# A linear-attention block beside a squared-ReLU layer: the last 64 query features taken from the keys' products, denominators by transposition

## The chip, the cores and the metric

The kernel runs on one core of a Trainium2 chip. A core has a matrix engine (TensorE, PE in the profile, with its weight loads as PEld), a vector engine (VectorE, DVE), a scalar engine (ScalarE, ACT), GpSimd (POOL) and a queue processor (SyncE, SP), which here only issues transfers. Each runs its own list of instructions in order and waits on semaphores for the others. Transfers are moved by 16 DMA engines. The metric is the device time of one execution in microseconds (us); lower is better.

## The reference, cut to what matters

There are S = 2048 rows x of D = 448 features. Two branches read the same x and are mixed by a gate per row:

```python
g = sigmoid((x * gate_w).sum(-1, keepdims=True))
# a: linear attention, 16 heads of 28 features
q, k, v = (x @ wqkv) split into three, each in 16 heads
phi = lambda t: where(t > 0, t + 1, exp(t)) + 1e-6
pq, pk = phi(q), phi(k)
kv  = einsum("hsd,hse->hde", pk, v)
z   = sum over s of pk                       # 28 sums for each head
num = einsum("hqd,hde->hqe", pq, kv)
den = einsum("hqd,hd->hq", pq, z) + 1e-6
a = (num / den) @ wo
# b: relu(x @ w1 + b1) ** 2 @ w2 + b2, 1792 hidden features
out = g * a + (1 - g) * b
```

## The kernel before

**Precision.** Operands are split into a high part, rounded for TensorE, and the low remainder; each product of matrices is two or three products on TensorE (high by high, high by low, low by high). The split is an ACT pass for the high part (`split_hi`, L65) and a VectorE subtraction for the low part (`split_lo`, L72). The 448 features fill three chunks of 128 partitions, and a fourth chunk of 64 carries high and low halves together, so a contraction over x takes 3 + 3 + 3 + 2 = 11 products.

**Order of the work.** The rows are four blocks (NB) of 512, each of four tiles of 128. Phase 1 walks blocks 0 to 3 and, for each, seven steps f of the hidden layer. A step does `up` (11 products of 512 columns, L229, into h_ps), `down` for the step before (12 products of 448 columns, L254, into o_ps) and one further piece: in steps 0 to 3 `keys` of one tile (11 products into k_ps, then phi in `first`, and splits and key sums in `rest`), in steps 4 to 6 `gram`, which sums phi(k) times x. Phase 2 walks the blocks in the order 3, 0, 1, 2, again in seven steps for the other half of the hidden layer. Its further pieces are `queries` (q_ps), the denominators, `scaled` (queries divided by them, and split), and `attention` (a_ps). In the first block of phase 2 also `kv_product` and `m_product` make the matrix m_s = kv times wo, whose parts are moved into place by transfers on POOL's queue (L442 to L444).

TensorE, ACT and VectorE keep the order in which the code calls them. Steps that use a finished product are put on the list `todo` and run at the start of the next step (`run_todo`). For SP and POOL a scheduler orders the instructions by when it reckons them ready. Most temporary tiles share 15 slots of the pool `work` (`slot`); a load waits on SP until its slot is free. Accumulators are banks of PSUM: `bank` alternates between two, h_ps and m_ps share two others, o_ps has four.

**Queries.** q_of puts 512 query features in four chunks of 128 partitions: 32 partitions for four heads. The last 64 features fill chunk 3 twice over, each once per half of a 32-group, so that high and low parts can be contracted together later (`split_last`). In `queries` chunks 0 to 2 take 11 products each and chunk 3 takes 7, whose result for half of a group lacks a low term; `swap` copies it out (L472), sends the halves of each 32-group to each other's place by 4 transfers on SP and 4 on POOL (L475), and `join` adds them. Chunk 3 is made first for a block, chunks 0, 1, 2 follow. After each chunk, phi gives pq, and ds gathers pq times zc, the key sums laid out by partition.

**Denominators.** `split_den` splits ds (dh, dl); `denominators` multiplies both by hm, a 128 x 128 mask that sums over the partitions of a head (d_ps, two products). ACT copies the result out with 1e-6 added (L494), and VectorE takes four reciprocals of 128 columns (L498).

**Key sums.** Each key tile's phi(k) is added up on POOL (L326) in ksum, [128 rows, 448]. `key_sums` puts it in the order of the query chunks (zk); in `kv_product` TensorE sums over the 128 rows with a column of ones (z_ps, four calls, eight products), and VectorE copies them to zc.

Of the kernel before, what the change touches and what calls it, by code (L numbers as in the profile page):

```python
# [30 lines left out]
def gated_mix_kernel(ctx: ExitStack, tc: tile.TileContext, xw, xt, xn, wk, wq, wv, wo, w1a, w1b, w2, b1, b2, gw,  # L31
                     hmask, kvmask, halves, out):
# [102 lines left out]
    def new_w1(h, g):  # L135
        n, a, z = ((TB, 0, 16), (3 * P, 48, 0))[g]
# [25 lines left out]

    wk_raw = {}

    def load_wk(c):
        wk_raw[c] = slot([P, D], F, f"wkr{c}")
        load(wk_raw[c], wk[c])
# [25 lines left out]
    ones = keep.tile([P, 2], F, name="ones")  # L193
    logit = keep.tile([P, NT], F, name="logit")
    gate = keep.tile([P, 2, NT], F, name="gate")
    zc = keep.tile([P, 4], F, name="zc")
# [10 lines left out]
    hm = keep.tile([P, 8 + P], R, name="hm")[:, 8:]  # L207
    dve.memset(ones, 1.0)
# [7 lines left out]
    hs = {}  # L216

# [72 lines left out]
    def keys(t, leave=0):  # L290
        b, i = divmod(t, 4)
        if t < 2:
            ps = (acc_p, mm_p)[t].tile([P, 512], F, name=f"k_ps{t}", tag=("acc", "mm")[t])
        else:
            ps = bank(f"k_ps{t}")
        terms = [term for c in range(4) for term in terms_x(*xs[b], slice(i * P, (i + 1) * P), wk_s, slice(0, D), c)]
        for n, (a, m) in enumerate(terms):
            owed.append((ps[:, :D], a, m, n == 0, n == len(terms) - 1))
# [48 lines left out]
    wq_s = keep.tile([P, 7 * TB], R, name="wq_s")  # L347
    wq_s = wq_s.rearrange("p (c n) -> p c n", c=7)
    wq_raw = {}

    def load_wq(c):
        wq_raw[c] = slot([P, TB], F, f"wqr{c}")
        load(wq_raw[c], wq[c])
# [3 lines left out]
    def split_wq(c):  # L357
        raw = wq_raw.pop(c)
        split_hi(act, wq_s[:, c], raw)
        if c < 3:  # L360
            split_lo(dve, wq_s[:, 4 + c, :384], raw[:, :384], wq_s[:, c, :384])
        else:
            split_lo(dve, wq_s[64:, 3, :384], raw[64:, :384], wq_s[64:, 3, :384])
        second = [t[:, 384:].rearrange("p (j r) -> p j r", j=NJ)[:, :, 16:] for t in (wq_s[:, c], raw)]
        split_lo(dve, second[0], second[1], second[0])
# [4 lines left out]
    zks = []  # L370

    def key_sums():
        zk = slot([P, 4, NJ, 32], F, "zk")
        ks = ksum.rearrange("p (j k) -> p j k", j=NJ)
        pool.memset(zk[:, 3], 0.0)
        pool.tensor_copy(zk[:, :3], ks[:, :, :96].rearrange("p j (c r) -> p c j r", c=3))
        pool.tensor_copy(zk[:, 3, :, :16], ks[:, :, 96:])
        zks.append(zk)
        act.activation(gate[:, 0], logit, AF.Exp, scale=-1.0)
        dve.tensor_scalar_add(gate[:, 0], gate[:, 0], 1.0)  # L380
        dve.reciprocal(gate[:, 0], gate[:, 0])
        dve.tensor_scalar(gate[:, 1], gate[:, 0], -1.0, 1.0, op0=ALU.mult, op1=ALU.add)
# [11 lines left out]
    def kv_product():  # L394
        kv_ps = bank("kv_ps")
        z_ps = mm_p.tile([P, 512], F, name="z_ps", tag="mm")
        for c in range(4):
            pe.matmul(z_ps[:, 2 * c:2 * c + 2], zks[0][:, c].rearrange("p j r -> p (j r)"), ones, start=True,  # L398
                      stop=True)
        dve.tensor_copy(zc, z_ps[:, 0:8:2])  # L400
# [31 lines left out]
    def m_product(j):  # L432
# [10 lines left out]
        pool.dma_start(out=m_s[p:p + 16, 3], in_=m[96:112, 0])  # L443
        pool.dma_start(out=m_s[p + 16:p + 32, 3], in_=m[112:, 1])  # L444


    pq, qs, den = {}, {}, {}

    def queries(b, c):
        ps = bank(f"q_ps{b}_{c}")  # L450
        xh, xl = xs[b]
        cols = slice(c * P, (c + 1) * P)
        if c < 3:
            products(ps, terms_w(xh, xl, wq_s, cols))
        else:
            products(ps, [(wq_s[:, i, cols], x[:, i]) for i in range(4) for x in ((xh, xl) if i < 3 else (xh,))])
        e = slot([P, TB], F, f"qe{b}_{c}")
        r = slot([P, TB], F, f"qr{b}_{c}")
        v = slot([P, TB], F, f"qv{b}") if c == 3 else None
        pq[b, c] = e  # L460

        def after():
            phi(ps if c < 3 else v, e, r, e)
# [5 lines left out]

        def swap():  # L470

            act.copy(v, ps)  # L472
            for p in range(0, P, 32):
                load(r[p:p + 16], v[p + 16:p + 32])
                pool.dma_start(out=r[p + 16:p + 32], in_=v[p:p + 16])  # L475
            return [join]

        def join():
            dve.tensor_tensor(v, v, r, op=ALU.add)
            after()  # L480
        return [swap if c == 3 else after]

    def split_den(b):
        den[b, "h"], den[b, "l"] = slot([P, TB], R, f"dh{b}"), slot([P, TB], R, f"dl{b}")
        total = den.pop((b, "s"))
        split_hi(act, den[b, "h"], total)
        split_lo(dve, den[b, "l"], total, den[b, "h"])

    def denominators(b):
        ps = bank(f"d_ps{b}")  # L490
        products(ps, [(hm, den.pop((b, "h"))), (hm, den.pop((b, "l")))])
        den[b, "r"] = rec = slot([P, TB], F, f"rec{b}")

        act.activation(rec, ps, AF.Copy, bias=1e-6)  # L494

        def part_(i):
            for j in range(2 * i, 2 * i + 2):
                dve.reciprocal(rec[:, j * P:(j + 1) * P], rec[:, j * P:(j + 1) * P])  # L498
        return [lambda: part_(0), lambda: part_(1)]

    def scaled(b, c):
        p = pq.pop((b, c))
        h = late.tile([P, TB], R, name=f"qh{b}_{c}", tag="q", bufs=NLATE)
        lo = late.tile([P, TB], R, name=f"ql{b}_{c}", tag="q", bufs=NLATE)
        qs[c] = (h, lo)
        dve.tensor_tensor(p, den[b, "r"], p, op=ALU.mult)
        if c < 3:
            split_hi(act, h, p)
            split_lo(dve, lo, p, h)
        else:  # L510
            split_last(h, lo, p, half)
# [18 lines left out]
    def run_todo():  # L530
        now, todo[:] = sorted(todo, key=lambda step: step.__name__ == "join"), []
# [33 lines left out]
    wk_s = keep.tile([P, 7, D], R, name="wk_s", tag="wkm", bufs=1)  # L565
# [53 lines left out]
    for b in range(1, NB):  # L619
        for f in range(NH):  # L620
# [36 lines left out]
            if b == 2:  # L657
# [4 lines left out]
                if f == 5:  # L662
                    raw = slot([P, P], F, "hmr")
                    pool.dma_start(out=raw, in_=hmask)
                    split_hi(act, hm, raw)
                    load(half, halves)
            if b == 3:
# [19 lines left out]
    for n, b in enumerate(order):  # L687
        then = order[n + 1] if n + 1 < NB else None
        for f in range(NF - NH, NF):
            fl = f - NH  # L690
            run_todo()
            if fl == (0 if n else 4) and n != 1:
                split_den(b)
            up(b, f)
            if then is not None and n and fl < 2:
# [32 lines left out]
            else:  # L728
                down(order[n - 1], NF - 1)
                for i in range(4):  # L730
                    if n == 1:
                        attention(order[0], i)
                        if i == 1:
                            split_den(b)
                    finish(order[n - 1], i)
            if n == 0:
                if fl in (2, 3):
                    m_product(fl - 2)
                if fl < 4:
                    todo += queries(b, (3, 0, 1, 2)[fl])  # L740
                if fl == 0:
# [5 lines left out]
                    m_s = keep.tile([P, 7, D], R, name="m_s", tag="wkm", bufs=1)  # L747
# [7 lines left out]
                for c in ((0,), (1, 2, 3))[fl - 5] if fl >= 5 else ():  # L755
                    scaled(b, c)
# [3 lines left out]
                if fl == 4:  # L760
                    todo += denominators(b)
            else:
                if fl == 0:
                    todo += denominators(b)
                if 2 <= fl < 4:
                    scaled(b, 2 * fl - 4)
                    scaled(b, 2 * fl - 3)
# [74 lines left out]
```

## Time and profile before

| | |
|---|---|
| device time, three runs | 434.67, 435.01, 435.04 us; median 435.01 |
| span of the profiled execution | 432.7 us |
| between span and median | 2.3 us |
| TensorE busy | 428.9 us, 2058 products |
| VectorE, ACT, POOL busy | 284.7, 174.8, 72.0 us |
| moved by DMA | 29.11 MB in 18411 packets |

The profile shows one execution. Busy times are unions of an engine's instructions. Matmuls are pipelined, so that their records overlap: the mean of a group is the duration of one product and not the distance from one to the next. That distance is read from the chain that ended last, which gives start, length and count of each run of products. A name such as "k_ps" stands for a tile with its buffer numbers left out; "L254" is a line of the kernel, which can be that of a helper.

### The profile page before, as it was taken

The page shows a single profiled execution, that of the slowest core. Times are in us where ns is not written, and L with a number is a line of the kernel's source. Part 1 is how long each engine was busy: PE and PEld are TensorE (multiplying, and loading weights), DVE is VectorE, ACT ScalarE, POOL GpSimd, SP SyncE. Part 2 cuts the span into 40 slices and gives each one's busy share as a digit, 9 for nine tenths or more (in the row PEclk, how much of TensorE's full clock was granted, in tenths as well). Part 3 has the DMA queues.
Part 4 walks back from the last instruction along what each step waited for, and adds up shares of the span by engine and source line. Part 5 has one row for each costly group of instructions (what it writes and reads, how often), then busy time and mean ns, then how long its engine had stood idle before and what let it go on. Part 6 is the DMA issues. An engine that isn't in the chain of part 4 may idle for free.

```text
span 432.7 us, 5576 instructions
## 1 busy us (share of the span) xinstructions
PE 428.9 (99%) x2058; PEld 380.6 (88%) x2058; DVE 284.7 (66%) x464; ACT 174.8 (40%) x304; POOL 72.0 (17%) x93
## 2 busy tenths in 40 slices
PE   9999999999999999999999999999999999999997
PEld 6889999898989899898898888988888888888986
DVE  5999518843499337884459777887653966457624
ACT  6855324521346133453145543444433534233421
POOL 0055006500065002540010441000100001000000
PEclk9999999999999999999999999999999999999999
DMA  8842302120232211223245321130101401002002
GB/s 284 240 134 63 96 0 71 24 68 5 65 89 63 68 45 48 66 59 110 65 117 144 72 63 38 63 120 0 26 0 46 139 0 27 0 0 86 0 2 85
DMA packets 18411, 29.11 MB, mean 67 GB/s; under 512 B 2896, under 2 KB 12736, under 8 KB 18384
## 3 DMA queue, kind: packets, MB, share of 16 engines
q1 hardware_dynamic: 16480, 26.46, 20.1%
q0 software_dynamic: 1760, 2.20, 2.3%
q8 instruction: 16, 0.26, 0.3%
q14 instruction: 11, 0.09, 0.1%
q10 hardware_dynamic: 144, 0.10, 0.1%
HBM read 22.43 MB, written 3.67 MB: 60 GB/s over the span
## 4 chain that ended last, share of the span: by engine, by line
PE 99%; DVE 0%; issue 0%
PE h_ps L229 32%; PE o_ps L254 31%; PE q_ps L84 8%; PE a_ps L84 8%; PE g_ps L84 8%; PE k_ps L254 8%; PE kv_ps L404 1%; PE warm_ps L177 1%; PE m_ps L84 1%; PE d_ps L84 0%; PE last L84 0%; PE h_ps L549 0%; PE z_ps L398 0%; DVE last L786 0%
## 5 line engine op out<-in xcount | busy, mean ns | idle before, releaser
L254 PE MATMUL o_ps<-w,hh 128*128 128x448 f32 x444 | 127.9, 362 | 0.0
L229 PE MATMUL h_ps<-xh,w 128*128 128x512 f32 x390 | 124.7, 390 | 0.0
L254 PEld LDWEIGHTS o_ps<-w,hh 128*128 128x128 f32 x444 | 83.2, 187 | 7.6
L229 PE MATMUL h_ps<-xl,w 128*128 128x512 f32 x224 | 86.7, 389 | 0.0
L229 PEld LDWEIGHTS h_ps<-xh,w 128*128 128x128 f32 x390 | 73.1, 188 | 14.7 <-DVE w L72 0.4
L254 PE MATMUL o_ps<-w,hl 128*128 128x448 f32 x222 | 80.4, 362 | 0.0
L233 ACT ACTIVATE hr<-h_ps,b_s 128x512 f32<-128x512 f32 x56 | 38.1, 680 | 85.8 <-PE h_ps L229 80.3
L69 DVE CAST hh<-hr 128x512 fp32r<-128x512 f32 x56 | 23.5, 420 | 61.3 <-ACT hr L234 61.1
L229 PEld LDWEIGHTS h_ps<-xl,w 128*128 128x128 f32 x224 | 42.0, 188 | 7.9
L254 PEld LDWEIGHTS o_ps<-w,hl 128*128 128x128 f32 x222 | 41.6, 188 | 3.7
L72 DVE TENSOR_TENSOR hl<-hr,hh 128x512 fp32r<-128x512 f32 x56 | 39.6, 707 | 3.4
L72 POOL TENSOR_TENSOR nl<-xnr,nh 128x384 fp32r<-128x384 f32 x16 | 17.2, 1075 | 119.0 <-ACT nh L65 118.9
L234 ACT ACTIVATE hr<-hr 128x512 f32<-128x512 f32 x56 | 35.4, 632 | 1.8
L84 PE MATMUL q_ps<-xh,wq_s 128*128 128x512 f32 x100 | 33.0, 389 | 0.0
L84 PE MATMUL a_ps<-m_s,qh 128*128 128x448 f32 x112 | 32.7, 362 | 0.0
L254 PE MATMUL k_ps<-wk_s,xh 128*128 128x448 f32 x112 | 32.7, 361 | 0.0
L475 POOL DMA_DIRECT2D qr<-qv x16 | 7.9, 503 | 124.3 <-ACT qv L472 94.5
L72 DVE TENSOR_TENSOR pl<-r,ph 128x448 fp32r<-128x448 f32 x16 | 23.7, 1479 | 0.0
L326 POOL TENSOR_TENSOR ksum<-ksum,r 128x448 f32<-128x448 f32 x15 | 23.3, 1554 | 1.1 <-DVE r L288 1.1
L84 PE MATMUL q_ps<-xl,wq_s 128*128 128x512 f32 x60 | 23.3, 389 | 0.0
L254 PE MATMUL k_ps<-wk_s,xl 128*128 128x448 f32 x64 | 23.2, 363 | 0.0
L84 PE MATMUL a_ps<-m_s,ql 128*128 128x448 f32 x64 | 23.2, 362 | 0.0
(118 smaller groups left out, 571.0 us busy)
## 6 DMA issues: line engine op xcount, KB each, us to landing
xr<-in_xt SPq DMA_DIRECT2D x27, 256.0 KB, 2.7
xnr<-in_xn SPq DMA_DIRECT2D x16, 224.0 KB, 2.6
out<-out SPq DMA_DIRECT2D x15, 224.0 KB, 2.0
w2r<-in_w SPq DMA_DIRECT2D x14, 224.0 KB, 2.7
w1r<-in_w1a SPq DMA_DIRECT2D x7, 256.0 KB, 2.8
w1r<-in_w1b SPq DMA_DIRECT2D x8, 192.0 KB, 3.3
m_s<-m POOLq DMA_DIRECT2D x12, 112.0 KB, 2.5
wqr<-in_wq SPq DMA_DIRECT2D x4, 256.0 KB, 2.7
```

The source lines that it names most:

```text
L69: eng.tensor_copy(hi, src)
L72: eng.tensor_tensor(lo, src, f32(hi), op=ALU.subtract)
L84: pe.matmul(out_ps, a, b, start=(i == 0), stop=(i == n - 1))
L177: pe.matmul(warm_ps[:, :256], warm[:, :P], warm, start=True, stop=True)
L229: pe.matmul(ps, a, m, start=(c == 0 and n == 0), stop=(c == 3 and n == 1))
L233: act.activation(r, ps, AF.Relu, bias=b1_s[:, f:f + 1])
L234: act.activation(r, r, AF.Square)
L254: pe.matmul(ps, a, m, start=start, stop=stop)
L326: pool.tensor_tensor(ksum, ksum, p, op=ALU.add)
L404: pe.matmul(kv_ps[:JE, js], wv_s[c][:, js], gsum[c][:, js], start=(c == 0), stop=(c == 3))
L475: pool.dma_start(out=r[p + 16:p + 32], in_=v[p:p + 16])
```

## The change

Four things are done in another way.

1. The weights of the last 64 query features stand beside the key weights: wk_s gets 512 columns in place of 448, and a key product gives a tile of rows by 448 key features and 64 query features. In `first`, VectorE transposes the 64 query columns in 32 x 32 blocks (tile q3), and SP writes the result to memory (q_d, 32 KB for each tile of rows). `load_v` later reads a block of 512 rows back, in four transfers in runs of 32 numbers (128 bytes), as a tile with features on partitions, each feature on two adjacent partitions. `queries` uses it as chunk 3. The seven products of chunk 3, `swap` and `join` are gone, and wq has 384 columns.
2. The partitions are permuted: a head's features lie on eight adjacent partitions in each chunk.
3. Denominators: ds is transposed on VectorE in 32 x 32 blocks, so that the eight partitions of a head become eight adjacent columns; VectorE reduces them to 64 columns, adds 1e-6 and takes one reciprocal of 64 columns; ACT spreads each over eight columns; VectorE transposes back. The mask hm and its products are gone.
4. Key sums: zk is transposed and reduced on VectorE, the result goes to memory in one transfer (zd) and comes back in four (z4), and `add_z`, one step later, adds the four parts into zc. z_ps is gone.

Chunk 3 comes last in a block of phase 2 (in the first block, first), `denominators` is called one step earlier or directly, and `scaled` does two chunks at a time with the first one's low part taken after the second one's multiplication. In the diff, whose cuts are lines of "...", some paddings of tiles are changed too.

```diff
     def load_wk(c):
-        wk_raw[c] = slot([P, D], F, f"wkr{c}")
+        wk_raw[c] = slot([P, TB], F, f"wkr{c}")
...
-        terms = [term for c in range(4) for term in terms_x(*xs[b], slice(i * P, (i + 1) * P), wk_s, slice(0, D), c)]
+        terms = [term for c in range(4) for term in terms_x(*xs[b], slice(i * P, (i + 1) * P), wk_s, slice(0, TB), c)]
...
         def first():
-            phi(ps[:, :D], e, r, p)
+            act.activation(e, ps[:, :D], AF.Exp)
+            dve.tensor_scalar(r, ps[:, :D], 0.0, 1e-6, op0=ALU.max, op1=ALU.add)
+            q = tmp.tile([P, 2, 32], F, name=f"q3_{t}", tag="q3", bufs=4)
+            dve.transpose(q.rearrange("p a s -> p (a s)"), ps[:, D:])
+            dve.scalar_tensor_tensor(p, e, 1.0, r, op0=ALU.min, op1=ALU.add)
+            qd = q_d[b].tile([4, P, 2, 32], F, name=f"qd{b}") if i == 0 else q_t[b]
+            q_t[b] = qd
+            load(qd[i], q)
...
     def key_sums():
-        zk = slot([P, 4, NJ, 32], F, "zk")
+        zk, zt = slot([P, NJ, 4, 32], F, "zk"), slot([P, 16, 32], F, "zt")
...
+        dve.transpose(zt.rearrange("p a s -> p (a s)"), zk.rearrange("p j c r -> p (j c r)"))
+        zr = zk.rearrange("p j c r -> p (j c r)")[:, :16]
+        dve.tensor_reduce(zr, zt, axis=mybir.AxisListType.X, op=ALU.add)
+        zd = z_d.tile([NJ, P, 4], F, name="zd")
+        load(zd.rearrange("j p c -> p j c"), zr.rearrange("p (j c) -> p j c", c=4))
+        for j in range(NJ):
+            load(z4[32 * j:32 * j + 32], zd[j].rearrange("(i r) c -> r i c", i=4))
+
+    def add_z():
+        dve.tensor_tensor(z4[:, :2], z4[:, :2], z4[:, 2:], op=ALU.add)
+        dve.tensor_tensor(zc, zc, z4[:, 1], op=ALU.add)
...
+    def load_v(b):
+        v = slot([P, TB], F, f"qv{b}")
+        rows = v.rearrange("(a r d) n -> a d r n", a=2, d=2)
+        for a in range(2):
+            for d in range(2):
+                load(rows[a, d].rearrange("r (t s) -> r t s", s=32), q_t[b][:, :, a].rearrange("t (i r) s -> r (t i) s", i=4))
+        vs[b] = v
...
     def denominators(b):
...
+        total, turned = den.pop((b, "s")), slot([P, TB], F, f"dt{b}")
+        dve.transpose(turned, total)
+        heads = total[:, :TB // 8]
+        dve.tensor_reduce(heads, turned.rearrange("p (h k) -> p h k", k=8), axis=mybir.AxisListType.X, op=ALU.add)
+        dve.tensor_scalar_add(heads, heads, 1e-6)
+        dve.reciprocal(heads, heads)
+        act.activation(turned.rearrange("p (h k) -> p h k", k=8), heads.unsqueeze(2).to_broadcast([P, TB // 8, 8]),
+                       AF.Copy)
+        den[b, "r"] = total
+        dve.transpose(total, turned)
...
+                if f == 4:
+                    load_v(b)
                 if f == 5:
                     key_sums()
+                    gates()
+                if f == 6:
+                    add_z()
...
-            if fl == (0 if n else 4) and n != 1:
-                split_den(b)
             up(b, f)
+            if n and fl == 1:
+                denominators(b)
+            if then is not None and n and fl == 2:
+                load_v(then)
...
+                if fl == 1:
+                    load_v(then)
...
                 if fl == 4:
-                    todo += denominators(b)
+                    denominators(b)
...
-                    todo += queries(then, (3, 0, 1, 2)[fl - 3])
+                    todo += queries(then, (0, 1, 2, 3)[fl - 3])
```

More of the change, by code (lines that the diff above doesn't have):

```diff
@@ L216, in gated_mix_kernel @@
     hs = {}
+    q_d = [ctx.enter_context(tc.tile_pool(name=f"q_d{b}", bufs=1, space=bass.MemoryType.DRAM)) for b in range(NB)]
+    q_t = {}
     def up_chunk(ps, b, f, c, only=None):
@@ L395, in kv_product @@
         kv_ps = bank("kv_ps")
[L396 to L400, printed above, removed]
         for j in range(NJ):
@@ L442, in m_product @@
             pool.dma_start(out=m_s[p:p + 32, c::4][:, :2], in_=m[c * 32:c * 32 + 32])
-        pool.dma_start(out=m_s[p:p + 16, 3], in_=m[96:112, 0])
-        pool.dma_start(out=m_s[p + 16:p + 32, 3], in_=m[112:, 1])
-    pq, qs, den = {}, {}, {}
-    def queries(b, c):
[L450 to L456, printed above, removed]
+        pool.dma_start(out=m_s[p:p + 32:2, 3], in_=m[96:112, 0])
+        pool.dma_start(out=m_s[p + 1:p + 32:2, 3], in_=m[112:, 1])
+    pq, qs, den, vs = {}, {}, {}, {}
+    def load_v(b):
[5 more added lines that the diff above has]
+        vs[b] = v
+    def queries(b, c):
         e = slot([P, TB], F, f"qe{b}_{c}")
         r = slot([P, TB], F, f"qr{b}_{c}")
-        v = slot([P, TB], F, f"qv{b}") if c == 3 else None
         pq[b, c] = e
+        if c == 3:
+            ps = vs.pop(b)
+        else:
+            ps = bank(f"q_ps{b}_{c}")
+            products(ps, terms_w(*xs[b], wq_s, slice(c * P, (c + 1) * P)))
         def after():
-            phi(ps if c < 3 else v, e, r, e)
+            phi(ps, e, r, e)
             if (b, "s") not in den:
@@ L468, in after @@
                 dve.scalar_tensor_tensor(den[b, "s"], e, zc[:, c:c + 1], den[b, "s"], op0=ALU.mult, op1=ALU.add)
[L470 to L487, printed above, removed]
@@ L489, in denominators @@
-    def denominators(b):
[L490 to L511, printed above, removed]
+        return [after]
@@ new lines, in scaled @@
+    def scaled(b, chunks):
+        owing = None
+        for c in chunks:
+            p = pq.pop((b, c))
+            h = late.tile([P, TB], R, name=f"qh{b}_{c}", tag="q", bufs=NLATE)
+            lo = late.tile([P, TB], R, name=f"ql{b}_{c}", tag="q", bufs=NLATE)
+            qs[c] = (h, lo)
+            dve.tensor_tensor(p, den[b, "r"], p, op=ALU.mult)
+            if owing:
+                split_lo(dve, *owing)
+            owing = None
+            if c < 3:
+                split_hi(act, h, p)
+                owing = lo, p, h
+            else:
+                split_last(h, lo, p, half)
+        if owing:
+            split_lo(dve, *owing)
@@ L530, in run_todo @@
     def run_todo():
-        now, todo[:] = sorted(todo, key=lambda step: step.__name__ == "join"), []
+        now, todo[:] = list(todo), []
         for step in now:
@@ L564, in gated_mix_kernel @@
     split_w2(1)
-    wk_s = keep.tile([P, 7, D], R, name="wk_s", tag="wkm", bufs=1)
+    wk_s = wide("wk_s")
     for c in range(4):
@@ L746, in gated_mix_kernel @@
                     late = ctx.enter_context(tc.tile_pool(name="late", bufs=1, side="right", reuse_waits="tile"))
-                    m_s = keep.tile([P, 7, D], R, name="m_s", tag="wkm", bufs=1)
+                    m_s = wide("m_s")[:, :, 16:16 + D]
                     split_kv(raw)
@@ L754, in gated_mix_kernel @@
                     m_product(3)
-                for c in ((0,), (1, 2, 3))[fl - 5] if fl >= 5 else ():
-                    scaled(b, c)
+                if fl >= 5:
+                    scaled(b, ((0, 1), (2, 3))[fl - 5])
                 if fl >= 4:
```

63 lines of the change are left out of this document (23 added, 40 removed).

## The prediction

> **What bounds the kernel now.** I read the page's busy times and slices first, then the waits of TensorE, then the chain that ended last in order of time.
>
> ```profile
> PE 428.9 (99%) x2058; PEld 380.6 (88%) x2058; DVE 284.7 (66%) x464; ACT 174.8 (40%) x304; POOL 72.0 (17%) x93
> ...
> DVE  5999518843499337884459777887653966457624
> ...
> PEclk9999999999999999999999999999999999999999
> ...
> PE 99%; DVE 0%; issue 0%
> ```
>
> ```profile
> PE warm_ps L177 <- PEq L834: 0.8, 1, 0.8
> ```
>
> TensorE's only recorded wait is the 0.8 us before its first instruction, its granted clock is full in every slice, and 99% of the chain is its own products. Nothing else delays the end. VectorE is full in slices 1 to 3, 11, 12 and 21, so it is close behind there, but TensorE does not wait for it. So a product taken away shortens the run by its own pitch, and new work elsewhere costs only once it makes TensorE wait.
>
> A matmul row's mean (389 ns for 512 columns) overlaps its neighbours, so the pitch has to come from the chain (start us, us, what):
>
> ```profile
> 23.79 2.49 PE h_ps L229 x11
> ...
> 28.69 2.20 PE k_ps L254 x11
> ...
> 215.09 1.59 PE q_ps L84 x7
> 216.68 0.79 PE z_ps L398 x8
> ...
> 351.00 1.59 PE q_ps L84 x7
> ...
> 388.47 0.45 PE d_ps L84 x2
> ```
>
> Eleven products of 512 columns take 2.49 us (0.226 each) and eleven of 448 columns 2.20 us (0.200 each). The seven-product q_ps pieces are the last query chunk, one per block: four in all, as are the d_ps pieces.
>
> **The change part by part: TensorE.** The profiled span is 432.7 us and the median run 435.01 us, so 2.3 us lie around the span; I keep these as they are.
> - Last query chunk out of `queries`: 4 x 1.59 = 6.36 us less.
> - Denominator products: 4 x 0.45 = 1.80 us less.
> - Key-sum products: 0.79 us less.
> - Key products widened from 448 to 512 columns, 11 for each of 16 tiles: 16 x (2.49 - 2.20) = 4.64 us more. The 512-column piece of L229 is the price, being the same count and form.
>
> Sum: 6.36 + 1.80 + 0.79 - 4.64 = 4.31 us less, a span of 428.4 us and a time of 430.7 us. What remains is whether any new wait reaches TensorE.
>
> **The change part by part: the cover.** Prices of the other engines:
>
> ```profile
> L72 DVE TENSOR_TENSOR pl<-r,ph 128x448 fp32r<-128x448 f32 x16 | 23.7, 1479 | 0.0
> L69 DVE CAST hh<-hr 128x512 fp32r<-128x512 f32 x56 | 23.5, 420 | 61.3 <-ACT hr L234 61.1
> L498 DVE RECIPROCAL rec<-rec 128x128 f32<-128x128 f32 x16 | 13.5, 908 | 0.9 <-ACT rec L494 0.9
> L479 DVE TENSOR_TENSOR qv<-qv,qr 128x512 f32<-128x512 f32 x4 | 2.8, 690 | 0.0
> L65 ACT ACTIVATE dh<-ds 128x512 fp32r<-128x512 f32 x4 | 2.5, 630 | 6.9 <-DVE ds L468 6.9
> L72 DVE TENSOR_TENSOR wq_s<-wqr,wq_s 128x64 fp32r<-128x64 f32 x4 | 1.7, 424 | 0.0
> L381 DVE RECIPROCAL gate<-gate 128x16 f32<-128x16 f32 x1 | 0.3, 252 | 0.0
> L415 DVE CAST kv_h<-kv_h 128x64 fp32r<-128x64 f32 x1 | 0.2, 189 | 0.0
> ```
>
> No row shows a transposition or a reduction on VectorE. For 512 columns I bound each by 0.42 us (the cast) and 1.48 us (the slowest full-width row) and take 0.69, the ordinary full-width operation. For 64 columns the ends are 0.19 and 0.42, and I take 0.3. Neither end is below zero: each is an added instruction. [...]
>
> *Phase 1.* Each of 16 key tiles adds a 0.3 us turn to VectorE between two operations of phi; 4.8 us in all, against 0.29 us more of TensorE's time per tile, so the balance of a step hardly moves. In block 2 the dropped second split of wq gives back 4 x 0.42. Behind a turn wait the rest of phi, its split and then the hidden layer's split. Where VectorE starts out full, the tightest place is:
>
> ```profile
> 24.41 0.74 DVE L72 TENSOR_TENSOR w<-w2r,w 128x448 fp32r<-128x448 f32 x1
> ...
> 26.12 0.37 PE L254 MATMUL o_ps<-w,hh 128*128 128x448 f32 x1
> ```
>
> The w2 split ends at 25.15 and is needed one product after 26.12. The wider wk splits (four, 64 columns more: 0.3 us by proportion) and one turn make it 0.6 us later; two key tiles make TensorE 0.6 us later too. With turns of 0.42 it still holds, as it does with wk arriving half a microsecond later for its extra 128 KB.
>
> *Denominators.* Per block, out go 0.69 of split and 3.6 of reciprocals on VectorE and two ACT passes; in come two turns, a reduction (2.07 together), a small add and a 64-column reciprocal (0.7 together, between the 16- and 128-column rows) and one ACT pass (0.63). VectorE and ACT get lighter by about 1.5 and 0.6 us. But the ACT pass now stands in ACT's queue behind a VectorE chain, and ahead of two x splits and the next block-step's relu. The tightest place is the third block of phase 2, step 1 to 3 (TensorE's chain first, then ACT and VectorE):
>
> ```profile
> 336.30 2.49 PE h_ps L229 x11
> ...
> 348.19 2.81 PE o_ps L254 x14
> ```
>
> ```profile
> 338.83 0.69 ACT L233 ACTIVATE hr<-h_ps,b_s 128x512 f32<-128x512 f32 x1 [1.89 <-PE h_ps L229]
> ...
> 340.09 1.14 ACT L65 ACTIVATE xh<-xr 128x512 fp32r<-128x512 f32 x2
> 343.53 0.69 ACT L233 ACTIVATE hr<-h_ps,b_s 128x512 f32<-128x512 f32 x1 [2.31 <-PE h_ps L229]
> ```
>
> ```profile
> 338.80 3.38 DVE L498 RECIPROCAL rec<-rec 128x128 f32<-128x128 f32 x4
> ...
> 345.45 0.69 DVE L72 TENSOR_TENSOR hl<-hr,hh 128x512 fp32r<-128x512 f32 x1
> ```
>
> Relu to split end takes 346.14 - 343.53 = 2.6 us. After the change: relu at 338.83, split done 341.4, turn and reduction 342.8, add and reciprocal 343.5, ACT pass 344.2, x splits 345.3, next relu (343.53 before) 345.3, its split done 347.9. TensorE reaches that down product at 348.19, with two owed products ahead of it, so the low half is needed near 349.0. About 1.1 us is left. With turn and reduction both at 1.48 the split is 1.6 us later and TensorE waits 0.5 us, in two blocks (the last loads no next x): 1.0 us, the upper end of this term. In the first block the denominators come two steps before their use, with more room.
>
> *Query chunk through memory.* Out go 4 ACT copies, 4 joins and 32 swap transfers, half of them on POOL's queue, where only the m_s transfers stay and wait for less. SP gets 16 writes of 32 KB, each waiting for a turn, and 16 reads. The reads are asked for three or four steps ahead of their use, over 25 us. The reads of block 3 follow its last write directly, so SP stands for about one landing; what is queued there (weights for phase 2) has several steps to go. Cost zero by this cover.
>
> *Key sums.* Turn and reduction follow the w2 split that ends at 199.4 on VectorE (the second fence here) and, at 0.69 each, are done near 200.8. Then come one write and four reads on SP, and `add_z` waits for them on VectorE.
>
> ```profile
> 198.99 0.83 SPq L58 DMA_DIRECT2D wv<-in_wv  x2
> ...
> 209.41 0.33 SPq L58 DMA_DIRECT2D w2r<-in_w  x1
> ```
>
> ```profile
> 198.84 0.62 DVE L72 TENSOR_TENSOR w<-w2r,w 128x448 fp32r<-128x448 f32 x1
> ...
> 208.77 0.61 DVE L72 TENSOR_TENSOR w<-w2r,w 128x448 fp32r<-128x448 f32 x1
> 209.83 0.62 DVE L344 TENSOR_TENSOR gsum<-g_ps,gsum 128x448 f32<-128x448 f32 x1 [0.44 <-PE g_ps L84]
> ```
>
> ```profile
> half<-in_halves SPq DMA_DIRECT2D x1, 1.0 KB, 6.2
> ```
>
> SP is free from 199.8 to 209.4. `add_z` is due at 209.4, so two transfers have 8.6 us. At 6.2 us each (the slowest landing here, also of a few bytes per partition) plus 1.6 us for issuing four, they end at 214.8. Behind `add_z` stands the last gsum, which the kv products need at 215.1 (216.68 and 217.46 move up, as q_ps and z_ps before them go): it would end at about 215.6, half a microsecond late. Landings like most loads' give nothing. Range 0 to 0.5.
>
> The remaining edits (narrower wq load, no mask load or its split, tile paddings, scaled's low half issued one chunk later, permuted rows) add no instruction to a tight place: zero.
>
> **The rivals.**
> *Small waits.* The terms above at their upper ends: 1.0 + 0.5, and up to twice that where several queues shift at once, give 431 to 434. For it: margins of about one microsecond. Against: VectorE's and ACT's load in phase 2 falls.
> *Slower: the 128-byte reads clog the transfer queue.* One block's reads are 2048 runs, 128 per DMA engine. In the first block of phase 2 they stand ahead of the next x chunks:
>
> ```profile
> 228.37 0.38 SPq L58 DMA_DIRECT2D w2r<-in_w  x1
> 232.93 2.24 SPq L58 DMA_DIRECT2D xr<-in_xt  x2
> ...
> 241.99 0.55 ACT L65 ACTIVATE m<-m_ps 128x448 fp32r<-128x448 f32 x1 [0.79 <-PE m_ps L84]
> ```
>
> ```profile
> 248.81 0.60 PE m_ps L84 x3
> ```
>
> ```profile
> q1 hardware_dynamic: 16480, 26.46, 20.1%
> ```
>
> That queue's packets took 0.201 x 16 x 432.7 / 16480 = 84 ns each, at 1.6 KB. Issued near 229, behind the w2 load, the runs end at 229 + 10.8 = 239.8 and x lands near 242.5. ACT then idles, but m_ps must leave its bank only before the second next product there, at 248.81; with some 2.5 us of ACT and VectorE work between, x may land until 246. From 146 ns a run (x at 250.4) the 4.3 us are gone; at 200 ns TensorE stalls 11 us and the time is 442. Against it: a shorter run should not cost more than a long one. [...]
> *No change.* The gain is eaten to within 0.2% (0.87 us): 3.4 to 5.2 us of waits, the same queues in between; about 435.
>
> **How the numbers follow.** Forecast 430.7 (430.1 to 431.3): 0.72. Small waits: 0.14, all still faster by over 0.2%, the bound a measurement of this kernel can tell. No change: 0.05. Slower: 0.09. So faster 0.86, same 0.05, slower 0.09. The range 430.0 to 433.0 holds the forecast and most of the small waits.
>
> **What would show it.** TensorE's chain should show no z_ps and d_ps, no x7 pieces of q_ps, and k_ps pieces of 2.49 us; TensorE's waits still next to nothing; transposes of 512 columns between 0.42 and 1.48 us. Idle TensorE after the down products of steps 2 and 3 in phase 2 would be the denominator chain; before kv_ps, the key sums; ACT waiting for x in the first block, the reads. If k_ps pieces take more than 2.49 us, the sum itself is wrong.

## The result and the profile after

The changed kernel takes 431.07 us (median of four runs, 430.75 to 431.32) against 435.02 us (434.67 to 435.2) for the kernel before beside it: a ratio of 0.9909, 95% interval 0.9897 to 0.9921. It is 3.95 us faster, where 4.3 us were forecast. The profiled execution took 431.32 us, its span 429.5 us.

From the page of the kernel after: busy times, TensorE's granted clock in 40 slices, and the chain's shares.

```profile
PE 424.9 (99%) x2014; PEld 373.0 (87%) x2014; DVE 279.5 (65%) x474; ACT 170.2 (40%) x295; POOL 64.1 (15%) x76
...
PEclk9999999999999999999999999999999999999999
...
PE 97%; DMA 1%; SPq 0%; ACT 0%; DVE 0%; issue 0%
```

The waits of TensorE after (us in total, times, longest):

```profile
PE warm_ps L180 <- PEq L837: 0.8, 1, 0.8
PE h_ps L234 <- ACT w L65: 0.3, 1, 0.3
PE h_ps L553 <- ACT w L65: 0.2, 1, 0.2
```

TensorE is still the bound at full clock. Its only new waits, half a microsecond, lie in the first 8 us, where it stands for the first weights. The chain after (start, length, what):

```profile
2.13 4.81 DMA w1r<-in_w1a
...
15.49 2.49 PE k_ps L259 x11
...
22.39 2.54 PE k_ps L259 x11
...
29.83 2.52 PE k_ps L259 x11
...
121.59 2.49 PE k_ps L259 x11
...
220.70 3.14 PE kv_ps L414 x32
...
275.55 8.80 PE a_ps L84 x44
...
426.29 0.42 DVE last L791
```

And three rows of the chain before that answer to them:

```profile
14.98 2.21 PE k_ps L254 x11
...
217.46 3.24 PE kv_ps L404 x32
...
429.71 0.42 DVE last L786
```

The chunk of seven products, z_ps and d_ps are gone from the chain. Two things differ from the forecast. A key piece takes 2.52 or 2.54 us rather than 2.49, except in tiles 0 and 9 (starts 15.49 and 121.59) and in tile 4, which runs in two parts of 2.04 and 0.45 us. And the first key piece starts 0.51 us later, since a load of the first weights landed later.

The start scatters, so I compare kernels below by the stretch from the first key piece to the end of the chain. Before: 429.71 + 0.42 - 14.98 = 415.15 us. After: 426.29 + 0.42 - 15.49 = 411.22 us. The difference is 3.93 us, close to that of the medians. The stretch leaves out what follows the chain's last instruction up to the end of the span: 432.7 - 430.13 = 2.6 us before and 429.5 - 426.71 = 2.8 us after, so the change loses some 0.2 us there.

### The profile page after: what moved, and what is told of

The parts are those of the page before. It is cut to its first block, busy times and chain, and to the rows that moved or that the text cites. A ratio compares the mean times of both kernels' runs of the same rounds, so it can differ in the third digit from the quotient of the medians.

```text
span 429.5 us, 5464 instructions
## 1 busy us (share of the span) xinstructions
PE 424.9 (99%) x2014; PEld 373.0 (87%) x2014; DVE 279.5 (65%) x474; ACT 170.2 (40%) x295; POOL 64.1 (15%) x76
## 4 chain that ended last, share of the span: by engine, by line
PE 97%; DMA 1%; SPq 0%; ACT 0%; DVE 0%; issue 0%
PE h_ps L234 32%; PE o_ps L259 31%; PE k_ps L259 9%; PE g_ps L84 8%; PE a_ps L84 8%; PE q_ps L84 7%; DMA w1r<-in_w1a 1%; PE kv_ps L414 1%; PE m_ps L84 1%; PE last L84 0%; SPq L58 0%; ACT w L65 0%; DVE last L791 0%
## 5 line engine op out<-in xcount | busy, mean ns | idle before, releaser
L259 PE MATMUL k_ps<-wk_s,xh 128*128 128x512 f32 x112 | 36.1, 392 | 0.0
L530 DVE SCALAR_TENSOR_TENSOR part<-part,gate,u 128x448 f32<-128x448 f32 x16 | 11.0, 685 | 26.2 <-ACT u L529 26.2
L84 PE MATMUL q_ps<-xh,wq_s 128*128 128x512 f32 x84 | 26.8, 389 | 0.0
L529 ACT ACTIVATE u<-a_ps,gate 128x448 f32<-128x448 f32 x16 | 10.2, 636 | 37.6 <-PE a_ps L84 37.6
L259 PE MATMUL k_ps<-wk_s,xl 128*128 128x512 f32 x64 | 25.0, 390 | 0.0
L259 PEld LDWEIGHTS k_ps<-wk_s,xh 128*128 128x128 f32 x112 | 21.0, 188 | 3.8
```

Source lines behind the costliest of these rows:

```text
L84: pe.matmul(out_ps, a, b, start=(i == 0), stop=(i == n - 1))
L259: pe.matmul(ps, a, m, start=start, stop=stop)
L529: act.activation(u, ps[:, :D], AF.Copy, scale=gate[:, 0, t:t + 1])
L530: dve.scalar_tensor_tensor(part[t], part[t], gate[:, 1, t:t + 1], u, op0=ALU.mult, op1=ALU.add)
```

## The experiments

| kernel | median, us | ratio to before (95%) | stretch, us | against the changed kernel's stretch |
|---|---|---|---|---|
| changed | 431.07 | 0.9909 (0.9897 to 0.9921) | 411.22 | |
| again | 431.31 | 0.9914 (0.9900 to 0.9927) | 411.23 | 0.0 |
| den_products | 432.69 | 0.9948 (0.9934 to 0.9961) | 413.03 | +1.8 |
| keysums_products | 437.39 | 1.0056 (1.0044 to 1.0069) | 418.01 | +6.8 |
| query_products | 435.08 | 1.0002 (0.9994 to 1.0011) | 414.96 | +3.7 |
| shift_32_bytes | 437.18 | 1.0053 (1.0040 to 1.0065) | 417.12 | +5.9 |
| keysums_in_place | 431.67 | 0.9926 (0.9913 to 0.9940) | 412.11 | +0.9 |
| query_in_place | 432.96 | 0.9957 (0.9944 to 0.9969) | 412.48 | +1.3 |
| shift_64_bytes | 434.95 | 1.0005 (0.9996 to 1.0014) | 415.34 | +4.1 |
| keys_256_bytes | 431.20 | 0.9914 (0.9900 to 0.9927) | 411.22 | 0.0 |
| keys_64_bytes | 431.84 | 0.9934 (0.9917 to 0.9950) | 411.87 | +0.7 |
| turns_late | 433.90 | 0.9977 (0.9967 to 0.9987) | 414.09 | +2.9 |
| reads_of_32_bytes | 430.76 | 0.9909 (0.9894 to 0.9924) | 411.22 | 0.0 |

### The same kernel again

> The changed kernel once more, unaltered. Theory one (the product count and pitch alone set the gain): the ratio of the first comparison returns, 3.5 to 4.5 us under the kernel before; key products again near 40.3 us in all, so the 0.42 us over the priced 40.0 is a property of the kernel. Rival (the 0.5 us by which the first key piece starts later in the changed kernel is caused by the change, through another order of landings at the start): the first key piece begins near 15.5 us again; if it is the chance of one execution, it begins near 15.0 and the span is 0.5 us shorter.

The chain of this execution:

```profile
14.83 2.49 PE k_ps L259 x11
...
425.64 0.42 DVE last L791
```

The stretch is the same to 0.01 us and the first key piece starts at 14.83. So the late start was one execution's chance, as the rival's second half had it: over all the profiles here the first key piece starts between 14.5 and 15.7 us. The slow key pieces return, so these belong to the kernel.

### Denominators by products again

```diff
-        dve.transpose(turned, total)
-        dve.tensor_reduce(heads, turned.rearrange("p (h k) -> p h k", k=8), axis=mybir.AxisListType.X, op=ALU.add)
...
+        products(ps, [(hm, den.pop((b, "h"))), (hm, den.pop((b, "l")))])
...
+            for j in range(2 * i, 2 * i + 2):
+                dve.reciprocal(rec[:, j * P:(j + 1) * P], rec[:, j * P:(j + 1) * P])
```

> The changed kernel with the denominators computed by mask products as before (two per block), the rest of the change kept. Theory one: the four pairs return, 4 x 0.45 = 1.80 us slower than the changed kernel, 432.9. Rival (the new chain of turn, reduction, ACT pass and turn makes TensorE wait somewhere): the undoing also takes that wait away, so that it costs less than 1.8, between 0.8 and 1.3 us, 431.9 to 432.4. A second rival (part of the gain was relief of VectorE, which the reciprocals of 128 columns load with 3.4 us per block): it costs more than 1.8, above 433.2.

The stretch grows by 1.81 us, the four pairs of 0.45 us and nothing more. The median's difference is 1.4 us beside `again`, within the scatter of the starts. Both rivals fall: no hidden wait went, and VectorE's reciprocals of 128 columns cost no time when they return.

### Two undoings that moved the operands

```diff
+    ones = keep.tile([P, 2], F, name="ones")
...
+        for c in range(4):
+            pe.matmul(z_ps[:, 2 * c:2 * c + 2], zks[0][:, c].rearrange("p j r -> p (j r)"), ones, start=True,
+                      stop=True)
```

> The changed kernel with the key sums by eight two-column products on TensorE as before, in place of the turn, the reduction and the round trip through memory. Theory one: 0.79 us slower than the changed kernel, 431.9. Rival (the round trip holds up add_z and the last gsum behind it): the products return but a wait goes, 0.3 us or less slower, 431.1 to 431.4.

```diff
-        terms = [term for c in range(4) for term in terms_x(*xs[b], slice(i * P, (i + 1) * P), wk_s, slice(0, TB), c)]
+        terms = [term for c in range(4) for term in terms_x(*xs[b], slice(i * P, (i + 1) * P), wk_s, slice(0, D), c)]
...
+            products(ps, [(wq_s[:, i, cols], x[:, i]) for i in range(4) for x in (xs[b] if i < 3 else xs[b][:1])])
```

> The changed kernel with the last query chunk by seven products of its own per block, and its pairs swapped by transfers as before; keys 448 columns wide again, no turns in phi, no 128-byte reads; the other two parts of the change are kept. Theory one: 4 x 1.59 = 6.36 us of products return and the key products lose 40.3 - 35.2 = 5.1 us, so 1.3 us slower than the changed kernel, 432.4 (432.8 by the 4.64 us of the forecast). Rival (the writes and the short reads cost something, or the turns in phi): the undoing takes that away, and the time is under 432.0, down to the changed kernel's 431.1.

Both missed by far, and on the far side of every theory: 6.1 and 3.8 us slower than `again`, where 0.8 and at most 1.7 were expected. No wait explains it: behind the first 10 us no wait of TensorE's products is recorded in either. What grew is the distance between products of lines that the edit does not touch. The chain with the key sums undone, and with the query chunk undone:

```profile
27.53 2.46 PE o_ps L261 x12
...
279.68 9.03 PE a_ps L84 x44
```

```profile
24.31 2.57 PE h_ps L234 x11
```

Twelve o_ps products took 2.41 us before and 44 of a_ps 8.80. Eleven h_ps took 2.49. Both edits also change the sizes of tiles, and with them the addresses in SBUF of everything allocated behind: by 32 bytes in the first; in the second, as compiled, the weights of the hidden layer's second group end up 64 bytes past a multiple of 256. The next two kinds of run take this apart. One thing is not as before in the second edit: the pairs are swapped by one transfer on SP and one on POOL a block, where the kernel before has four and four.

### Only the place moved

```diff
-    keep.tile([P, 8 + P], R, name="off")
+    keep.tile([P, 16 + P], R, name="off")
```

> The changed kernel with the unused tile eight floats longer and nothing else: all tiles of TensorE that are allocated behind it lie 32 bytes further on, the slots of the hidden layer stay. Theory one (TensorE's pitch hangs on where the operands lie): 5 us slower than the changed kernel, about 436.3, without a single new wait, by o_ps pieces of 2.46 us for twelve products and h_ps of 2.52 for eleven. Rival (placement has no effect and the slower pitch of keysums_products had another cause): 431.1.

It is 5.9 us slower in the stretch, where 5 were expected, and its median 6.0 above that of keys_256_bytes, which ran beside it: an unused tile that is eight floats longer costs more than the whole change brings. The chain:

```profile
34.92 2.46 PE o_ps L259 x12
...
278.70 9.03 PE a_ps L84 x44
```

TensorE's only recorded wait is the 0.8 us ahead of its first instruction, as before. Only the pitch grows, from 0.201 to 0.205 us for o_ps; the pieces of eleven h_ps take 2.52 us on average, though from 2.49 to 2.56 by what stands before them. Placement has the effect, and the rival falls.

### The two undoings in place

The column of ones now stands inside the unused tile; the query variant gets the 192 bytes of padding of the kernel before. Each cut shows only what differs from the undoing above.

```diff
-    keep.tile([P, 8 + P], R, name="off")
-    ones = keep.tile([P, 2], F, name="ones")
+    ones = keep.tile([P, 8 + P], F, name="off")[:, :2]
```

> As keysums_products (key sums by eight two-column products), but the column of ones stands inside the unused tile, so that every operand of TensorE lies at the address that it has in the changed kernel; in keysums_products the two extra floats had moved all later tiles by 32 bytes. Theory one (the 6.1 us of keysums_products are 0.8 us of products and 5.3 us of slower pitch by placement): 0.79 us slower than the changed kernel, 431.9, with o_ps pieces of twelve back at 2.41 us and h_ps pieces at 2.49. Rival (the key sums on TensorE themselves cost 6 us, by a stall or a displaced order): 437 again.

```diff
-        n, a, z = ((TB, 0, 16), (3 * P, 0, 0))[g]
+        n, a, z = ((TB, 0, 16), (3 * P, 48, 0))[g]
```

> As query_products (last query chunk by its own seven products, keys 448 columns), with the 192 bytes of padding ahead of the second half of the hidden weights that the kernel before has, so that TensorE's operands lie at the addresses of the kernel before. Theory one (product pitch): 1.3 us slower than the changed kernel, 432.4, h_ps pieces back from 2.53 to 2.49 and q_ps pieces from 2.52 to 2.49. Rival (the short reads, writes and turns make room when they go, or the swap transfers cost): a time off 432.4 by more than half a microsecond, with all pieces at 2.49.

The chain with the key sums undone in place, then with the query chunk undone in place:

```profile
27.15 2.41 PE o_ps L260 x12
...
220.43 0.79 PE z_ps L406 x8
```

```profile
22.22 2.20 PE k_ps L259 x11
24.42 2.49 PE h_ps L234 x11
...
215.72 1.59 PE q_ps L84 x7
```

The pitches are back, and the key sums with the two floats in the wrong place are 418.01 - 412.11 = 5.90 us slower than in place, just what shift_32_bytes costs. The stretches grow by 0.89 (0.79 of products and 0.10 that kv_ps takes longer behind them) and 1.26 us (6.36 - 5.06 = 1.30 expected). The three undoings add up to 1.81 + 0.89 + 1.26 = 3.96 us; the change brought 3.93. So the gain is products counted at their pitch, as the first theory has it, and the round trips through memory neither cost nor bring anything in the stretch. One thing is left over: the median of the query variant lies 1.8 us above that of keys_256_bytes beside it, 0.5 more than its stretch does; its five runs reach from 432.61 to 433.88. By the median alone the rival's sign, over half a microsecond off 432.4 with the pieces at 2.49, is just met (432.96); by the stretch it is not. About half of the 0.5 us lies behind the chain: from its last instruction to the end of the span it takes 431.1 - 428.09 = 3.0 us here and 429.4 - 426.67 = 2.7 in keys_256_bytes. What fills that time the profile does not show, and the rest is within the scatter of the starts.

### Which places are bad

```diff
-    keep.tile([P, 8 + P], R, name="off")
+    keep.tile([P, 24 + P], R, name="off")
```

> The changed kernel with the unused tile 16 floats longer than there, so that the tiles behind it lie 64 bytes further on, where shift_32_bytes moved them by 32. Theory one (what counts is that an operand's row starts on a multiple of 64 bytes): the pitch of the changed kernel returns, 431.1, o_ps pieces of twelve at 2.41 and h_ps at 2.49. Rival (what counts is how far the streamed and the loaded operand lie apart, modulo some larger step): o_ps and a_ps, whose loaded operand stays in its slot, get slower, h_ps and q_ps, whose both sides move, keep 2.49; over 431.1 by up to the 4 us that o_ps and a_ps lost in shift_32_bytes.

The chain:

```profile
34.80 2.45 PE o_ps L259 x12
...
49.99 2.51 PE h_ps L234 x11
...
277.55 8.98 PE a_ps L84 x44
```

Neither theory holds. Multiples of 64 bytes are not enough: the kernel is 4.1 us slower in the stretch. The rival is right that o_ps and a_ps, with one side moved, get slower, but h_ps and q_ps are slower in part too: eleven h_ps take 2.51 to 2.54 us behind g_ps pieces and 2.49 behind k_ps pieces, eleven q_ps 2.50 to 2.54.

```diff
-        return keep.tile([P, 48 + 7 * TB], R, name=name, tag="wkm", bufs=1)[:, 48:].rearrange("p (c n) -> p c n", c=7)
+        return keep.tile([P, 112 + 7 * TB], R, name=name, tag="wkm", bufs=1)[:, 112:].rearrange("p (c n) -> p c n", c=7)
```

> The changed kernel with the key weights 256 bytes further on in their tile. Theory one (the 2.52 us of the key pieces, 0.03 over the price of 2.49, come from where the weights lie against x: 72448 bytes apart, an odd multiple of 256, where the weights of h_ps lie 32768 apart): key pieces of 2.49 us, 0.3 to 0.4 us faster in all, 430.7. Rival (the form, with x as the stationary side, has this price): pieces stay at 2.52 and the time at 431.1.

Nothing moved: the key pieces are 2.54 and 2.52 us as before and the stretch is 411.22.

```diff
-        return keep.tile([P, 48 + 7 * TB], R, name=name, tag="wkm", bufs=1)[:, 48:].rearrange("p (c n) -> p c n", c=7)
+        return keep.tile([P, 64 + 7 * TB], R, name=name, tag="wkm", bufs=1)[:, 64:].rearrange("p (c n) -> p c n", c=7)
...
```

Two further lines of this edit keep the other operands where they were: 192 bytes of padding ahead of the hidden weights' second group, and m_s taken from its tile 64 bytes earlier.

> The changed kernel with the key weights 64 bytes in place of 0 past a multiple of 256, as all weights streamed in 448 columns lie; the other operands stay where they were, modulo 256. Theory one (the 2.52 us of a key piece come from where the key weights begin): 2.49 us, 0.3 to 0.4 us faster in all, 430.7. Rival (the pieces' price comes from the order of products ahead of them, as the pieces of tiles 0 and 9, at 2.49 in the same kernel, suggest): 2.52 on average again, 431.1. Third outcome, since h_ps pieces with loaded weights 64 bytes off went to 2.53 in query_products: slower, 2.53 to 2.57, up to 0.8 us.

The chain with the keys 64 bytes on:

```profile
29.46 2.52 PE k_ps L259 x11
31.98 2.54 PE h_ps L234 x11
...
47.19 2.40 PE g_ps L84 x12
49.59 2.49 PE h_ps L234 x11
```

The key pieces take 40.37 us in all against 40.29, and of the 0.65 us that the kernel loses 0.59 lie in h_ps: a piece takes 2.51 to 2.54 us right behind a key piece and 2.49 behind g_ps. As compiled, h_ps has the same operand addresses in keys_256_bytes, to the byte, and takes 2.49 behind k_ps there. Of what runs ahead of those pieces only the key weights lie elsewhere. So the distance between these products depends also on which products ran just before, and on their operands. That speaks for the rival's mechanism, but not for its sign: the pieces of tiles 0 and 9 take 2.53 us here, and the time is not 431.1. The third outcome has the size, but by h_ps and not by the key pieces. What sets the rhythm, and why most key pieces start in a slow one, stays open.

### The denominators' cover, spent

```diff
-        dve.transpose(turned, total)
+        for _ in range(4):
+            dve.transpose(turned, total)
```

> The changed kernel with the first turn of the denominators made four times over instead of once (the same result), so that in each block the ACT pass, the x splits and the next relu come 3 x 0.705 = 2.1 us later. Theory one (the forecast's tightest place, with some 1.2 us left): TensorE waits about 0.85 us after the down products of step 2 in the second and third block of phase 2, where the next block's x is split too, and not in the others; 1.7 us in all, about 432.9. Rival (the cover there is wider than the forecast says): no wait, 431.1. Second rival (there was no cover left, the chain already sits on the path): 2.1 us in three or four blocks, 437 or more.

The waits of TensorE's weight loads, the rows on the hidden layer, and the loads in the second block of phase 2 (start, length; in brackets the idle time before):

```profile
PEld o_ps L259 <- DVE hh L69: 2.0, 2, 1.0
PEld o_ps L259 <- DVE hl L72: 1.3, 3, 0.5
```

```profile
296.32 0.30 PEld L259 LDWEIGHTS o_ps<-w,hh 128*128 128x128 f32 x2 [1.01 <-DVE hh L69]
297.12 0.19 PEld L259 LDWEIGHTS o_ps<-w,hl 128*128 128x128 f32 x1 [0.50 <-DVE hl L72]
```

TensorE waits in the place that the forecast named, after step 2, where the next x is split, in two blocks. A third wait in the last block is small (0.2 us). The stretch grows by 2.87 us, some 1.3 in each of the two blocks where 0.85 was expected: the place of the first theory is right, its size missed. Three turns in a row took 2.2 us, and TensorE lost 1.3 of them, so the cover was about 0.9 us, not 1.2. Both rivals fall.

### Shorter runs

```diff
-                load(rows[a, d].rearrange("r (t s) -> r t s", s=32), q_t[b][:, :, a].rearrange("t (i r) s -> r (t i) s", i=4))
+                for k in range(0, 32, 8):
+                    load(rows[a, d].rearrange("r (t s) -> r t s", s=32)[:, :, k:k + 8],
+                         q_t[b][:, :, a].rearrange("t (i r) s -> r (t i) s", i=4)[:, :, k:k + 8])
```

> The changed kernel with each read of the query chunk cut into four, of 32-byte runs in place of 128-byte ones: 8192 runs a block and 16 issues on SP instead of 2048 and 4, the same bytes to the same places. Theory one (the reads are hidden, asked for steps ahead of their use): 431.1 to 431.5, no new wait of TensorE. Rival (the runs clog the queue by their number, 84 ns each over 16 engines: 43 us a block): x of the next block and the weights behind them come late in the first block of phase 2, 10 us slower or more; at a quarter of that price, 21 ns a run, some 11 us a block, still hidden.

From this kernel's DMA view: the main queue (packets, MB, share of 16 engines' span), and the reads (count, KB each, us to landing):

```profile
q1 hardware_dynamic: 53168, 27.40, 24.0%
...
qv<-qd SPq DMA_DIRECT2D x64, 16.0 KB, 2.4
```

And the queue's row of `again`, which has the same bytes in fewer packets:

```profile
q1 hardware_dynamic: 27824, 27.40, 21.4%
```

Four times as many runs cost nothing; the stretch is 411.22. The queue's packets took 0.240 x 16 x 428.6 = 1646 us against 0.214 x 16 x 428.8 = 1468, or 178 us more for 25344 more packets: 7 ns each, a twelfth of the rival's 84. The trace's packet records give the price of a run itself: 12.7 ns on average for the 8192 runs of 128 bytes in the kernel after, 8.3 for the 32768 of 32 bytes here. So the reads of the change were far from clogging anything.

## Why the prediction was right, step by step

The forecast was 430.7 us with 430.0 to 433.0 around it; the kernel takes 431.07. The forecast case came true, 0.4 us short of its sum.

**Removed products: right.** The undoings return 1.81 us for d_ps (1.80 in the sum), 0.89 for z_ps (0.79, and 0.10 of kv_ps behind it), and the q_ps pieces of seven are 1.59 us in the undoing as in the sum.

**Key products: the term that was mis-sized.** "The 512-column piece of L229 is the price, being the same count and form" gave 4.64 us. The 18 key pieces add up to 40.29 us after and 35.23 before: 5.06 us, 0.42 more. The count and the shapes are the same, but the roles are not: h_ps streams x past loaded weights, k_ps streams the weights past loaded x. The role alone does not set the price either, since tiles 0, 4 and 9 take 2.49 us; why the others take 2.52 or 2.54 stays open. By the forecast's own last sign, key pieces above 2.49 us, its sum was off in this term. The sum with this term is -3.89, with kv_ps -3.99; measured -3.93.

**Paddings at zero: right in value, wrong in reason.** They were put at zero since they "add no instruction to a tight place". The runs show that a shift of 32 bytes costs 5.9 us without an instruction. In the compiled programs before and after, the operands of h_ps, o_ps, q_ps and a_ps begin at the same places modulo 256 bytes, and their pitch stayed (in both, twelve o_ps take 2.41 us, 44 a_ps 8.80, eleven h_ps or q_ps 2.49 or 2.50 but for one h_ps piece); moved as in shift_32_bytes, the change ends slower than the kernel before. The forecast did not look at this, so in this term it was lucky. None of the rivals held it.

**Prices of the new operations: right.** The groups of the kernel after, busy us and mean ns of one behind the bar:

```profile
L319 DVE STREAM_TRANSPOSE q<-k_ps 128x64 f32<-128x64 f32 x16 | 3.8, 238 | 0.0
...
L488 DVE STREAM_TRANSPOSE dt<-ds 128x512 f32<-128x512 f32 x4 | 2.8, 705 | 0.0
L490 DVE TENSOR_REDUCE ds<-dt 128x64 f32<-128x512 f32 x4 | 2.7, 686 | 0.1
L493 ACT ACTIVATE dt<-ds 128x512 f32<-128x512 f32 x4 | 2.5, 632 | 13.0 <-DVE ds L492 13.0
L492 DVE RECIPROCAL ds<-ds 128x64 f32<-128x64 f32 x4 | 2.2, 554 | 0.1
L491 DVE TENSOR_SCALAR ds<-ds 128x64 f32<-128x64 f32 x4 | 0.8, 195 | 0.1
```

A turn of 512 columns was taken as 0.69 us and is 0.705; the reduction 0.69 and 0.686; the small turn 0.3 and 0.238; add and reciprocal 0.7 and 0.75; the ACT pass 0.63 and 0.632. The two turns measured here lie 0.705 - 0.238 = 0.467 us apart for 448 columns, 1.04 ns a column. By an estimate from these two, some 0.17 us of a turn do not depend on its width, if reading PSUM (the small turn) and SBUF (the large one) costs the same, which no run shows. The row of the trace before from which the price was taken, 0.690 us, came within 0.015 us of the large turn.

**Cover of the denominators: right place, margin slightly smaller.** ACT and VectorE in the third block of phase 2, after, the down products that wait for them in the chain, and TensorE's first load of the new low half:

```profile
342.19 0.63 ACT L493 ACTIVATE dt<-ds 128x512 f32<-128x512 f32 x1 [3.38 <-DVE ds L492]
...
343.77 0.67 ACT L238 ACTIVATE hr<-h_ps,b_s 128x512 f32<-128x512 f32 x1
```

```profile
345.67 0.69 DVE L72 TENSOR_TENSOR hl<-hr,hh 128x512 fp32r<-128x512 f32 x1
```

```profile
346.82 2.81 PE o_ps L259 x14
```

```profile
347.27 0.19 PEld L259 LDWEIGHTS o_ps<-w,hl 128*128 128x128 f32 x1
```

The low half is ready at 346.36. Down starts at 346.82 with two owed products ahead, and the low half is loaded at 347.27: 0.9 us are left, as turns_late measures. "About 1.1 us is left" was the forecast; it put that load 0.8 us behind the start of the piece, and it comes 0.45 behind it.

**Key sums: no wait.** VectorE behind the round trip, after:

```profile
214.38 0.61 DVE L72 TENSOR_TENSOR w<-w2r,w 128x448 fp32r<-128x448 f32 x1
214.91 0.16 DVE L390 TENSOR_TENSOR z<-z 128x8 f32<-128x8 f32 x1
...
215.44 0.62 DVE L356 TENSOR_TENSOR gsum<-g_ps,gsum 128x448 f32<-128x448 f32 x1 [0.17 <-PE g_ps L84]
```

`add_z` starts right behind its neighbour, and the last gsum waits for its own product, not for `add_z`. It ends at 216.06 and kv_ps starts at 220.70. The upper bound of 0.5 us was not needed: the write landed in 2.8 us and each read in 2.1 (median), where the bound took 6.2 for either, and over 4 us of room were left.

**Reads: hidden.** SP issues them at 230.46 and x behind them at 236.21; ACT splits that x at 243.13 without an idle time before it (none stands in the row):

```profile
230.46 2.62 SPq L58 DMA_DIRECT2D qv<-qd  x4
236.21 0.83 SPq L58 DMA_DIRECT2D xr<-in_xt  x2
```

```profile
243.13 0.62 ACT L65 ACTIVATE xh<-xr 128x512 fp32r<-128x512 f32 x1
```

**The rivals.** Small waits did not come: no wait of TensorE remains outside the start. The slower case needed 146 ns a run of 128 bytes, and one took 12.7.

**Two readings that were off without effect.** VectorE is full in slice 31 of the kernel before too (335 to 346 us), which the forecast did not list; that slice covers most of the place that it named as the tightest. And of the 2.3 us put around the span some 0.5 are the difference between the profiled execution and the median run: time and span of one execution lie 1.8 us apart (431.32 and 429.5). Both sides of the forecast hold the same 2.3, so it falls out.

## What to carry to other kernels

Where one engine has no waits, count its instructions at the pitch read from the chain: three undoings added up to the gain within 0.03 us, in the stretch that they were read from. But the pitch of h_ps, 2.49 us for eleven products, came out as 2.52 or 2.54 in most key pieces, so leave a margin when a pitch is moved to another tile. And before an experiment adds or drops a tile, compare the addresses of the matrix engine's operands: two floats in the wrong place cost 5.9 us here without a wait, which could pass for the price of the products that they served.

## What the runs showed of the hardware

- **Placement in SBUF changed TensorE's pitch.** With tiles 32 bytes further on, twelve o_ps products take 2.46 us in place of 2.41 and 44 a_ps products 9.03 in place of 8.80; with 64 bytes, 2.45 and 8.98. In both runs the granted clock is full in every slice, and the only recorded wait of the products is the 0.8 us ahead of the first. What in the addresses decides was not found.
- **Pitch also differed with the products just before.** Key pieces take 2.49 us in tiles 0, 4 and 9 and 2.52 or 2.54 elsewhere, and the same three tiles are the quick ones in both profiles of the changed kernel. Eleven h_ps with the same addresses take 2.51 to 2.54 us behind key pieces whose weights begin 64 bytes past a multiple of 256, and 2.49 behind key pieces whose weights begin on one.
- **Very short runs were cheap in this queue.** A read of 512 runs of 32 bytes lands in 2.4 us (median of 64), one of 512 runs of 128 bytes in 2.6 (median of 16). Splitting the runs in four added 7 ns of a DMA engine's time for each packet more, and nothing to the kernel's time.
